# A transformer block on one core: layernorm tile 5 transposed by DMA, two tiles' statistics as sums, and a new order of the opening and the loop

## The chip, the cores and the metric

The kernel runs on one core of a Trainium2 chip. The time is the device time of one execution in microseconds; the median of three executions before the change is 274.92 us (274.09 to 275.06). The engines are called by their names or by the profile's short ones: TensorE (PE for matmuls, PEld for its weight loads), VectorE (DVE), ScalarE (ACT), GpSimd (POOL) and SyncE (SP), which here only issues DMAs.

## The reference

One block of a transformer over S = 2048 tokens of width D = 640, all in bf16: layernorm, a linear attention with 32 heads of width 20 and a softmax feature map, a residual, a second layernorm and a gated FFN of width 1536 with a second residual.

```python
def _A_ref(x, wqkv, w_phi, wo):
    qkv = ((x @ wqkv).reshape(B, S, 3, H, Dh)).transpose(2, 0, 3, 1, 4)
    q, k, v = qkv[0], qkv[1], qkv[2]
    pq = jnp.einsum("bhsd,hdf->bhsf", q, w_phi)
    pk = jnp.einsum("bhsd,hdf->bhsf", k, w_phi)
    phi_q = concat([softmax(pq), softmax(-pq)], axis=-1)
    phi_k = concat([softmax(pk), softmax(-pk)], axis=-1)
    kv = jnp.einsum("bhsf,bhsd->bhfd", phi_k, v)
    z  = jnp.einsum("bhsf->bhf", phi_k)
    num = jnp.einsum("bhqf,bhfd->bhqd", phi_q, kv)
    den = jnp.einsum("bhqf,bhf->bhq", phi_q, z)[..., None] + 1e-6
    return (num / den).transpose(0, 2, 1, 3).reshape(B, S, D) @ wo

h = x + _A_ref(layernorm(x), wqkv, w_phi, wo)
out = h + (gelu(layernorm(h) @ w_gate) * (layernorm(h) @ w_up)) @ w_down
```

## The kernel before

The tokens lie in 16 tiles of 128 (`t` = 0 to 15). Everything stays on the core; weights and x come in once, the result goes out once. The work of each engine, and of SyncE's DMA queue, stands in the order in which the kernel's calls are written: there is no planner. An engine does its own instructions strictly in that order and waits in front of each until its inputs are there; what is written earlier for another engine holds it only through data or through a buffer.

The stages, and the short names in which the calls are written:

- **Opening.** `load_x`, `load_v`, `load_phi`, `load_T` put x, the v weights, w_phi and the transposed q and k weights on SyncE's queue. `warm` and `warms` keep TensorE running on zeros. Tiles 0 to 2 are transposed with the mean taken off only (`c_sum`, `c_xc`, `c_sq`, `c_rstd`: the sum, the centred tile, the sum of squares, and rstd, which is put in later as a scale). Later tiles get `bn` (`bn_stats` of one half, with the aggregate after the second half), `rt` (rstd, on GpSimd with a power or on ScalarE with Ln and Exp), `mr` (minus mean times rstd), and `ap` (the normalized tile, on VectorE or ScalarE).
- **Transposes of the normalized tiles** into `LN1T`: `tr` makes five 128x128 transposes on TensorE into PSUM and `tc_` copies them out; `dt` instead puts one DMA transpose on SyncE's queue.
- **Folded weights.** `bd` makes the block diagonal of w_phi (`BD`); `fm(i, d)` multiplies chunk d of the q (i = 0) or k (i = 1) weights with it on TensorE, and `fc` casts the result into `Wq2` or `Wk2`.
- **Loop over the tiles.** `vm` makes v (ten matmuls of 128x320), `ve` evicts it; `km` makes pk, `ke(t, 0)` and `ke(t, 1)` its two exponentials on ScalarE; `ks` sums them per head on VectorE, `kr` takes the reciprocal, `kx(t, s, e)` scales v by it on VectorE ("v") or GpSimd ("g") into `vt`; `kv` adds 40 small matmuls per tile into the PSUM sum `kvp`. `kv_clear` builds a mask on GpSimd in pieces, `kv_mask` takes `kvp` out.
- **q side and attention.** `qm` and `qe` make the features of q; `ab`, `ae`, `a_den`, `a_rec`, `a_w`, `a_o` the attention of a tile; `o_tr`/`o_tc` or `o_dt` transpose it, `po_` projects it, `res` adds the residual.
- **FFN.** `gu`, `gl`, `gm` make gate and up, the GELU and their product, `dn` the down projection, `da` the last sum, `so` the store. `load_w` brings the weights for it.

Matmul results of all stages share four PSUM buffers. `gtile` hands them out in the order of the written calls, first freed first used, and `give` returns one after the call that reads it out. So which eviction a matmul group waits for follows from the written order of both. From the first `kv` to `kv_mask` one of the four holds `kvp`.

Lines 665 to 734 are the opening up to the second `bd`. VectorE's order there is: sums and centred tiles 0 to 2, the copies of tiles 0 and 1, `bn(3, 0)`, `bn(3, 1)`, the copy of tile 2 (`tc_(2, 0, 5)`), which `vm(2)` needs.

Of the kernel before, what the change touches and what calls it, by code (L numbers as in the profile page):

```python
# [8 lines left out]
BF16 = mybir.dt.bfloat16  # L9
# [8 lines left out]
def kernel(  # L18
# [76 lines left out]
    def eq_tiles(pool, j0, j1):  # L95
# [12 lines left out]
    tmean, trstd = (const.tile([P, 4], F32, name=n) for n in ("tmean", "trstd"))  # L108
# [16 lines left out]
    junk = fp.tile([P, D], BF16, name="junk")  # L125
# [6 lines left out]
    def col(x, t):  # L132
        return x[:, t:t + 1]
# [21 lines left out]
    def load_x(t0, t1):  # L155
        nc.sync.dma_start(x_sb[t0 // 4][:, t0 % 4:t0 % 4 + t1 - t0, :], x_v[:, t0:t1, :])  # L156
        have.update(("x", t) for t in range(t0, t1))
# [161 lines left out]
    def warmed():  # L319
        give(wu)  # L320
# [371 lines left out]
    load_x(10, 12)  # L692
    warm(0, 0)
# [40 lines left out]
    bd(3, 5, "g")  # L734
# [10 lines left out]
    vm(1, 4, 5)  # L745
    ve(1)
    vm(2)
    warmed()
    ap(3, "v")
    tr(3)  # L750
    bn(5, 0)
    bn(5, 1)
    rt(5, 1, "g")
    kv_clear(1)
    kv_clear(2)
    tc_(3, 0, 5, "v")
    bn(4, 0)
    bn(4, 1)
    ve(2)
    fm(1, 1)  # L760
    fc(1, 1, "a")
    fm(1, 0)
    fc(1, 0, "a")
    ap(5, "v")
    rt(4, 1, "a")
    ap(4, "v")
    vm(3)
    ve(3)
    tr(5)
    tc_(5, 0, 5, "v")  # L770
# [3 lines left out]
    fc(1, 3, "v")  # L774
    tr(4)
    fm(1, 4)
# [3 lines left out]
    tc_(4, 0, 5, "v")  # L780
    km(4)
    ke(4, 1)
    ke(4, 0)
    ke(0, 1)
    km(1)
    ke(0, 0)
    ke(1, 1)
    km(3)
    ke(3, 1)
    ke(1, 0)  # L790
    km(2)
# [36 lines left out]
    ke(7, 1)
    load_T(0, 4)
    dt(6)  # L830
    dt(9)
    load_T(0, 3)
    mr(8)
    ap(8, "a")
    km(5)
    ve(7)
    mr(10)
    ap(10, "a")
    dt(8)
    dt(10)  # L840
    vm(6, by_chunk=False)
    km(6)
    ke(7, 0)
    ke(5, 0)
    ve(6)
    ke(6, 0)
    vm(9, by_chunk=False)
    km(9)
    kr(0)
    kx(0, 1, "g")  # L850
    c_late(0, 3)
    ke(5, 1)
    mr(11)
    ks(2)
    kr(1)
    kx(1, 1, "g")
    kx(1, 0, "g")
    ve(9)
    ke(6, 1)
    kv(1)  # L860
    bn(12, 0, 2)
    bn(13, 0, 2)
    kr(2)
    bn(12, 1, 2)
    bn(14, 0, 2)
    bn(13, 1, 2)
    rt(12, 2, "g")
    kx(2, 0, "v")
    ap(0, "v")
    dt(0)  # L870
    load_T(0, 0)
    load_T(0, 2)
    load_T(0, 1)
    kx(0, 0, "g")
    kv(0)
    ke(9, 0)
    fm(0, 3)
    fc(0, 3, "a")
    ks(3)
    kr(3)  # L880
    kx(3, 0, "g")
    bn(15, 0, 2)
    ks(4)
    ks(5)
    kr(4)
    bn(15, 1, 2)
    mr(12)
    ap(12, "a")
    vm(8, by_chunk=False)
    ve(8)  # L890
    ke(9, 1)
    dt(12)
    kx(3, 1, "g")
    kx(2, 1, "g")
    kx(4, 1, "g")
    ap(13, "v")
    dt(13)
    km(8)
    ke(8, 1)
    ap(11, "a")  # L900
    dt(11)
    kr(5)
    bn(14, 1, 2)
    ks(6)
    kr(6)
    kx(6, 1, "v")
    kx(5, 0, "g")
    rt(14, 2, "g")
    mr(14)
    kx(5, 1, "g")  # L910
    kx(4, 0, "g")
    mr(15)
# [154 lines left out]
    load_w("o", 2, 5)  # L1067
# [507 lines left out]
```

## Time and profile before

| | |
|---|---|
| median of 3 runs | 274.92 us |
| the profiled execution's own time | 274.87 us |
| its span, first to last instruction | 273.2 us |
| granted TensorE clock | 1.000 |
| busy: VectorE, ScalarE, GpSimd | 178.1, 135.6, 89.3 us |
| DMA packets, bytes | 43392, 21.62 MB |

A page of the profile gives for each engine its busy time, then the span in 40 slices of 6.8 us with the busy share in tenths, then the chain of work that ended last, followed back from the last instruction. "A <- B" names what released an instruction. The time lines list instructions as start, length, engine, line, operation, output and inputs, shapes and count; what stands in brackets is the idle time in front and what ended it. Where "x2" stands, start and length are of both together.

### The profile page before, as it was taken

What the parts mean: (1) busy time and instruction counts of PE and PEld (TensorE: products, weight loads), DVE (VectorE), ACT (ScalarE), POOL (GpSimd) and SP (SyncE); (2) the same over time, 40 slices, a digit from 0 to 9 for tenths busy, and PEclk for the clock granted to TensorE, in tenths of its full rate; (3) what the DMA queues carried; (4) which work ended last, traced back from release to release, by engine and by line L of the source; (5) the groups of instructions that cost most, each with busy time, mean ns of one, the idle gap of its engine ahead of it and who ended that gap; (6) DMA issues with size and microseconds to landing.
All of it is one profiled execution on the core that took longest, in us unless ns stands there. A gap on an engine that the chain in (4) does not pass through costs nothing.

```text
span 273.2 us, 7140 instructions
## 1 busy us (share of the span) xinstructions
PE 268.7 (98%) x2981; PEld 171.0 (63%) x2981; DVE 178.1 (65%) x333; ACT 135.6 (50%) x236; POOL 89.3 (33%) x212
## 2 busy tenths in 40 slices
PE   8999999999999999999999999999999999999995
PEld 4777777766455887788755545675554576444574
DVE  6799999997586786676487855974457403233413
ACT  5968998859699665254704333422315340222200
POOL 4678999689003104342400320420201140000000
PEclk9999999999999999999999999999999999999999
DMA  6963878970780141321213021064001713000002
GB/s 199 198 236 75 118 101 90 230 282 2 234 303 3 26 28 26 73 52 24 52 26 96 2 48 27 0 124 50 0 0 48 122 48 97 2 0 1 24 2 96
DMA packets 43392, 21.62 MB, mean 79 GB/s; under 512 B 35936, under 2 KB 41312, under 8 KB 43360
## 3 DMA queue, kind: packets, MB, share of 16 engines
q1 hardware_dynamic: 43360, 21.17, 35.3%
q8 instruction: 23, 0.38, 0.6%
q14 instruction: 9, 0.07, 0.1%
HBM read 10.18 MB, written 2.62 MB: 47 GB/s over the span
## 4 chain that ended last, share of the span: by engine, by line
PE 95%; DMA 2%; SPq 1%; DVE 1%; issue 0%
PE gu L619 38%; PE pd L644 19%; PE pq L446 8%; PE po L546 8%; PE pk L377 8%; PE pv L330 7%; PE ab L491 2%; PE kvp L418 2%; DMA x_sb<-in_A_x_dram 2%; PE wa L356 1%; PE tp L150 1%; SPq L156 0%; DVE stats L260 0%; SPq L160 0%; DVE LN1T L130 0%
## 5 line engine op out<-in xcount | busy, mean ns | idle before, releaser
L625 ACT ACTIVATE g<-gu 128x512 bf16<-128x512 f32 (+1 forms) x60 | 29.7, 511 | 70.6 <-PE gu L619 70.1
L632 DVE TENSOR_TENSOR GT<-gu,g 128x512 bf16<-128x512 f32 (+1 forms) x60 | 33.9, 581 | 47.2 <-ACT g L625 47.2
L619 PE MATMUL gu<-LN2T,Wg 128*128 128x512 bf16 (+1 forms) x300 | 61.8, 337 | 0.0
L619 PE MATMUL gu<-LN2T,Wu 128*128 128x512 bf16 (+1 forms) x300 | 61.8, 337 | 0.0
L644 PE MATMUL pd<-Wd,GT 128*128 128x320 bf16 (+2 forms) x396 | 54.0, 296 | 0.0
L644 PEld LDWEIGHTS <-GT 128*128 128x128 bf16 x396 | 37.5, 98 | 14.3 <-DVE GT L632 0.3
L619 PEld LDWEIGHTS <-Wu 128*128 128x128 bf16 x300 | 29.3, 98 | 22.6
L619 PEld LDWEIGHTS <-Wg 128*128 128x128 bf16 x300 | 28.9, 98 | 22.0
L403 POOL TENSOR_TENSOR vt<-vS,rs 128x672 bf16<-128x672 bf16 x23 | 30.3, 1344 | 4.3 <-DVE rs L397 4.0
L654 DVE TENSOR_TENSOR y<-pd,x_sb 128x640 bf16<-128x640 f32 (+3 forms) x18 | 13.1, 744 | 23.5 <-PE pd L644 23.4
L524 DVE TENSOR_TENSOR tt<-AB,w 128x1280 bf16<-128x1280 f32 x16 | 23.8, 1490 | 1.2 <-POOL w L518 0.9
L546 PE MATMUL po<-Wo,oT 128*128 128x320 bf16 x160 | 24.2, 300 | 0.0
L330 PE MATMUL pv<-Wv,LN1T 128*128 128x320 bf16 x160 | 24.0, 300 | 0.1
L377 PE MATMUL pk<-Wk,LN1T 128*128 128x320 bf16 x160 | 23.4, 300 | 0.0
L446 PE MATMUL pq<-LN1T,Wq 128*128 128x512 bf16 x100 | 23.3, 380 | 0.0
L393 DVE TENSOR_REDUCE sk<-E 128x64 f32<-128x1280 bf16 x16 | 22.9, 1451 | 0.3 <-ACT E L384 0.3
L450 ACT ACTIVATE Eq<-pq 128x1024 bf16<-128x1024 f32 (+1 forms) x26 | 20.0, 851 | 4.9 <-PE pq L446 4.9
L580 POOL TENSOR_SCALAR v<-sm 128x1 f32<-128x1 f32 x14 | 4.9, 348 | 53.3 <-DVE x_sb L567 51.4
L546 PEld LDWEIGHTS <-oT 128*128 128x128 bf16 x160 | 15.5, 98 | 6.9 <-ACT oT L130 0.2
L130 ACT COPY AB<-ab 128x704 f32<-128x704 f32 x19 | 13.6, 743 | 12.4 <-DVE tt L524 9.8
L384 ACT ACTIVATE E<-pk 128x640 bf16<-128x640 f32 x26 | 17.4, 712 | 4.2 <-PE pk L377 3.2
L330 PEld LDWEIGHTS <-LN1T 128*128 128x128 bf16 x160 | 15.3, 98 | 6.6 <-DVE LN1T L130 0.7
(104 smaller groups left out, 286.9 us busy)
## 6 DMA issues: line engine op xcount, KB each, us to landing
out_dram<-y SPq DMA_DIRECT2D x15, 160.0 KB, 2.0
x_sb<-in_A_x_dram SPq DMA_DIRECT2D x6, 320.0 KB, 4.7
Wu<-in_B_w_up_dram SPq DMA_DIRECT2D x5, 384.0 KB, 8.2
Wg<-in_B_w_gate_dram SPq DMA_DIRECT2D x5, 384.0 KB, 4.6
Wd<-in_B_w_down_dram SPq DMA_DIRECT2D x4, 480.0 KB, 8.0
x_sb<-in_A_x_dram SPq DMA_DIRECT2D x4, 160.0 KB, 3.2
Wv<-in_A_wqkv_dram SPq DMA_DIRECT2D x2, 320.0 KB, 4.4
Wo<-in_A_wo_dram SPq DMA_DIRECT2D x1, 480.0 KB, 8.0
```

Source lines behind the costliest of these rows:

```text
L330: nc.tensor.matmul(pv[t][:, u, 0:HD], lhsT=lnT(t, c), rhs=Wv[:, c, u * HD:(u + 1) * HD], start=(c == 0), stop=(c == NC - 1))
L377: nc.tensor.matmul(pk[t][:, u, 0:HD], lhsT=lnT(t, c), rhs=Wk2[:, c, u * HD:(u + 1) * HD], start=(c == 0), stop=(c == NC - 1))
L393: nc.vector.reduce_sum(sk[t], Ek[t].rearrange("p s (h f) -> p (s h) f", f=Dh), axis=AX.X)
L403: E[e].tensor_tensor(Vt[t][:, s], vS[t % 8], rs[t][:, s * H:(s + 1) * H, None].to_broadcast([P, H, VC]), ALU.mult)
L446: nc.tensor.matmul(pqs[j][:, i, :], lhsT=Wq2[:, kc, c * P:(c + 1) * P], rhs=LN1T[b][:, kc, :], start=(kc == 0), stop=(kc == NC - 1))
L450: nc.scalar.activation(Eq[j][:, :, s, :], pqs[j][:, 0:len(QG[j])], ACTF.Exp, scale=(1.0, -1.0)[s])
L524: nc.vector.tensor_tensor(tt.rearrange("p s (h f) -> p s h f", f=Dh), num, w[t][:, :, :, None].to_broadcast([P, 2, H, Dh]), ALU.mult)
L546: nc.tensor.matmul(po[t][:, u, 0:HD], lhsT=oT[t][:, c, :], rhs=Wo[:, c, u * HD:(u + 1) * HD], start=(c == 0), stop=(c == NC - 1))
L619: nc.tensor.matmul(p[:, i, 0:a1 - a0], lhsT=W[:, c, f * P:(f + 1) * P], rhs=LN2T[b][:, c, a0:a1], start=(c == 0), stop=(c == NC - 1))
L625: nc.scalar.activation(x[:, 0:a1 - a0], p[:, 0, 0:a1 - a0], ACTF.Gelu_apprx_tanh)
L632: nc.vector.tensor_tensor(GT[b, f][:, a0:a1], p[:, 1, 0:a1 - a0], x[:, 0:a1 - a0], ALU.mult)
L644: nc.tensor.matmul(pd[k][:, u, n0:n1], lhsT=GT[b, f][:, tl * P:(tl + 1) * P], rhs=Wd[:, f, u * HD + n0:u * HD + n1], start=(f == 0), stop= ...
```

## The change

Four things change. Tile 5 is transposed by DMA (`dt(5)`) and no longer on TensorE. The statistics of tiles 12 and 13 come from a sum (ScalarE for 12, VectorE for 13) and a sum of squares on ScalarE, with a new function `sr` on GpSimd for their mean and rstd; the small buffers for it become 16 columns wide, and `junk`, which these passes write, moves to the pool `p1`. The second part of `bd` moves from GpSimd to VectorE. And the calls from there to the first `gu` stand in a new order for all engines, some on another engine. Nothing else of the computation changes.

The tiles and the new function:

```diff
-    tmean, trstd = (const.tile([P, 4], F32, name=n) for n in ("tmean", "trstd"))
+    tmean, trstd = (const.tile([P, NT], F32, name=n) for n in ("tmean", "trstd"))
...
+    junk = p1.tile([P, D], BF16, name="junk")
     tsum, tsq, tlog, nrstd, prstd = (
-        p1.tile([P, 4], F32, name=n) for n in ("tsum", "tsq", "tlog", "nrstd", "prstd"))
+        p1.tile([P, NT], F32, name=n) for n in ("tsum", "tsq", "tlog", "nrstd", "prstd"))
...
-    junk = fp.tile([P, D], BF16, name="junk")
...
+    def sr(t0, t1):
+
+        need(*(("sq", t) for t in range(t0, t1)))
+        n = t1 - t0
+        ve, rstd = small(p1, [P, n], "ve1"), small(p1, [P, n], "rstd1")
+        nc.gpsimd.tensor_scalar(ve, tsq[:, t0:t1], 1.0 / (D * D * D), EPS, op0=ALU.mult, op1=ALU.add)
+        nc.gpsimd.tensor_tensor(rstd, ve, nhalf[:, 0:n], op=ALU.pow)
+        nc.gpsimd.tensor_scalar(tmean[:, t0:t1], tsum[:, t0:t1], 1.0 / D, None, op0=ALU.mult)
+        for j in range(n):
+            lnp[t0 + j] = [col(tmean, t0 + j), rstd[:, j:j + 1], None]
```

The opening and the beginning of the loop, before and after, one call after the other (calls on one line stand in this order):

```diff
-    bd(3, 5, "g")
+    bd(3, 5, "v")
     c_sq(2); c_rstd(2, 3); bn(3, 0); bn(3, 1); rt(3, 1, "a"); tr(2); tc_(2, 0, 5, "v")
     vm(0, 2, 4); vm(0, 4, 5); ve(0); vm(1, 4, 5)
-    ve(1); vm(2); warmed(); ap(3, "v"); tr(3); bn(5, 0); bn(5, 1); rt(5, 1, "g")
-    kv_clear(1); kv_clear(2); tc_(3, 0, 5, "v"); bn(4, 0); bn(4, 1); ve(2)
-    fm(1, 1); fc(1, 1, "a"); fm(1, 0); fc(1, 0, "a"); ap(5, "v"); rt(4, 1, "a"); ap(4, "v")
-    vm(3); ve(3); tr(5); tc_(5, 0, 5, "v"); fm(1, 2); fc(1, 2, "a"); fm(1, 3); fc(1, 3, "v")
-    tr(4); fm(1, 4); fc(1, 4, "a"); km(0, True); loop_pools(); tc_(4, 0, 5, "v")
-    km(4); ke(4, 1); ke(4, 0); ke(0, 1); km(1); ke(0, 0); ke(1, 1); km(3); ke(3, 1)
-    ke(1, 0); km(2); ke(2, 1); vm(4); ve(4); ke(2, 0); bn(7, 0); bn(7, 1); bn(6, 0)
+    warmed(); bn(5, 0); ap(3, "v"); bn(5, 1); bn(4, 0); ve(1); vm(2); ve(2); bn(4, 1)
+    rt(4, 1, "a"); fm(1, 0); fc(1, 0, "v"); ap(4, "v"); tr(3); tc_(3, 0, 5, "v")
+    fm(1, 1); fc(1, 1, "a"); fm(1, 2); fc(1, 2, "a"); fm(1, 3); fc(1, 3, "a")
+    tr(4); tc_(4, 0, 5, "v"); kv_clear(1); kv_clear(2); bn(7, 0); bn(7, 1); bn(6, 0)
+    rt(5, 1, "g"); ap(5, "v"); rt(7, 1, "g"); dt(5); bn(6, 1); rt(6, 1, "g"); kv_clear(3)
+    ap(7, "v"); bn(8, 0, 2); bn(9, 0, 2); bn(8, 1, 2); dt(7); kv_clear(4); ap(6, "v")
+    bn(9, 1, 2); rt(8, 2, "g"); mr(8); mr(9); fm(1, 4); fc(1, 4, "a"); km(0, True)
+    loop_pools(); ke(0, 1); ke(0, 0); ks(0); km(2); ke(2, 1); ke(2, 0); km(1); ke(1, 1)
+    ke(1, 0); km(4); ke(4, 1); c_sum(12, "a"); vm(4); ve(4); ke(4, 0); ks(1); kr(1)
+    kx(1, 1, "g"); km(3); ke(3, 0); c_sq(12); ap(8, "a"); ke(3, 1); vm(3); ap(9, "a")
...
```

The rest of the loop after the change, engine by engine (the orders that the text refers to):

```
TensorE: km(5) vm(5) km(7) fm(0,3) vm(6) vm(7) km(6) fm(0,1) km(9) fm(0,4) kv(0) kv(1) kv(2) vm(9)
         km(8) km(10) vm(10) km(13) vm(13) kv(3) kv(4) kv(5) vm(12) vm(8) km(12) vm(11) km(11)
         kv(6) kv(7) vm(15) fm(0,2) km(15) vm(14) fm(0,0) km(14) qm(2) qm(0) kv(9) kv(8) kv(12)
         qm(3) qm(1) kv(15) kv(10) kv(13) kv(11) kv(14) qm(4) ab(0)
VectorE: ... bn(9,1) ks(0) ks(1) kr(1) bn(10,0) bn(11,0) bn(11,1) bn(10,1) ks(2) kr(0) kr(2) c_sum(13)
         fc(0,3) bn(14,0) ks(4) bn(15,0) ks(3) ap(13) kr(4) bn(15,1) ks(5) kr(3) bn(14,1) kr(5) ks(7)
         ap(0) ks(9) ks(8) kx(4,1) kx(5,1) kr(7) ks(6) kr(8) kr(9) kr(6) ap(1) ks(13) ks(10) ks(12) ...
GpSimd:  ... mr(8) mr(9) kx(1,1) kx(1,0) rt(10) mr(10) kx(0,0) kx(2,1) sr(12,14) kx(0,1) kx(2,0) mr(11)
         mr(12) kx(4,0) c_late kx(3,0) kx(5,0) rt(14) kx(3,1) mr(14) mr(15) kx(7,1) kx(7,0) kx(9,1)
         kx(6,1) kx(6,0) kx(9,0) ...
ScalarE: ... ve(5) ve(3) ke(5) c_sq(13) ap(10) ve(6) ve(7) ke(7) fc(0,1) ke(9) fc(0,4) ap(12) ke(6) ve(9) ...
SyncE:   x loads, dt(5) dt(7) load_T(0,3) dt(6) load_w(g,3,4) load_w(u,0,1) load_T(0,1) load_T(0,4)
         dt(8) dt(9) load_w(g,2,3) load_w(o,2,5) dt(10) dt(13) dt(12) load_w(u,2,3) dt(0) load_T(0,2)
         dt(11) load_w(u,1,2) load_T(0,0) dt(15) dt(14) dt(1) load_w(g,1,2) dt(2) load_w(u,4,5)
         load_w(u,3,4) load_w(o,0,2) load_w(g,4,5) load_w(d,3,6) load_w(g,0,1) o_dt(2) load_w(d,9,12)
         load_w(d,6,9) load_w(d,0,3)
```

The two x loads of tiles 12 to 15 are written before the loop now; on SyncE's queue they stood directly behind the other x loads already. In the attention stage `a_den(1)` goes from VectorE to GpSimd, the two evictions of `ab(0)` and of `ab(3)` change engines with one another, and `ab(3)` stands ahead of the first `gu`.

More of the change, by code (lines that the diff above doesn't have):

```diff
@@ L773 @@
     fm(1, 3)
-    fc(1, 3, "v")
+    fc(1, 3, "a")
     tr(4)
+    tc_(4, 0, 5, "v")
+    kv_clear(1)
+    kv_clear(2)
+    bn(7, 0)
+    bn(7, 1)
+    bn(6, 0)
+    rt(5, 1, "g")
+    ap(5, "v")
+    rt(7, 1, "g")
+    dt(5)
+    bn(6, 1)
+    rt(6, 1, "g")
+    kv_clear(3)
+    ap(7, "v")
+    bn(8, 0, 2)
+    bn(9, 0, 2)
+    bn(8, 1, 2)
+    dt(7)
+    kv_clear(4)
+    ap(6, "v")
+    bn(9, 1, 2)
+    rt(8, 2, "g")
+    mr(8)
+    mr(9)
     fm(1, 4)
@@ L846 @@
+    ap(13, "v")
+    dt(10)
+    kx(2, 0, "g")
+    mr(11)
+    mr(12)
+    ap(12, "a")
     ke(6, 0)
+    kv(1)
+    kv(2)
     vm(9, by_chunk=False)
[L848 to L870 removed]
@@ L885 @@
[L885 to L888, printed above, removed]
+    bn(14, 1, 2)
+    kr(5)
+    kx(5, 0, "g")
+    ks(7)
+    rt(14, 2, "g")
+    ap(0, "v")
+    dt(12)
+    load_w("u", 2, 3)
+    dt(0)
+    kx(3, 1, "g")
+    mr(14)
+    kv(3)
+    ks(9)
+    ks(8)
+    kx(4, 1, "v")
+    kv(4)
+    kx(5, 1, "v")
+    kv(5)
+    ke(13, 1)
+    ke(13, 0)
+    vm(12, by_chunk=False)
+    mr(15)
+    ap(15, "a")
+    ve(13)
+    ve(12)
+    ap(14, "a")
     vm(8, by_chunk=False)
     ve(8)
-    ke(9, 1)
```

449 lines of the change are left out of this document (209 added, 240 removed).

## The prediction

> **What bounds the kernel now.** I read the page first (busy times and the 40 slices), then the list of who waited for whom on TensorE, then the chain of waits in order of time, and last the time lines of VectorE, ScalarE, GpSimd and SyncE over the opening and the loop.
>
> ```profile
> PE 268.7 (98%) x2981; PEld 171.0 (63%) x2981; DVE 178.1 (65%) x333; ACT 135.6 (50%) x236; POOL 89.3 (33%) x212
> PE   8999999999999999999999999999999999999995
> PEclk9999999999999999999999999999999999999999
> ```
>
> The last wait of TensorE in the list of waits:
>
> ```profile
> PE ab L491 <- issue: 0.2, 1, 0.2
> ```
>
> TensorE is busy in every slice, at full granted clock, and after its start it waited once, 0.2 us in the attention stage. A busy TensorE need not be at its peak, so the chain of waits has to confirm it.
>
> ```profile
> 3.17 4.76 DMA x_sb<-in_A_x_dram
> ...
> 7.95 0.90 DVE stats L260 x2
> ...
> 9.08 0.36 DVE LN1T L130
> ...
> 9.49 1.53 PE pv L330 x10
> 11.03 0.28 PE tp L150 x5
> 11.30 0.65 PE wa L356 x12
> 11.95 1.47 PE pv L330 x10
> ...
> 14.65 0.32 PE wa L356 x6
> 14.97 6.79 PE pk L377 x50
> ...
> 33.99 0.79 PE kvp L418 x73
> 34.78 0.42 PE wa L356 x6
> 35.20 1.36 PE pv L330 x10
> ```
>
> Up to 9.49 us the start hangs on the load of x tile 3, its two `bn_stats` and the copy of tile 2. From there the chain stays on TensorE to the end: ten 128x320 matmuls take 1.36 us again and again, with no gap. So a microsecond that TensorE loses in the opening is lost for good, and another engine that gets faster gives nothing. What the edit can gain is TensorE work taken away, and that is five transposes (0.28 us).
>
> The other engines have little to spare in the loop:
>
> ```profile
> 20.00:30.00 10.00, 10.00 (x75) 7.21 (x74) 9.83 (x21) 9.30 (x14) 9.04 (x24) 1.00 0.52 71
> 30.00:40.00 10.00, 10.00 (x153) 7.31 (x151) 9.83 (x16) 9.77 (x18) 9.40 (x10) 1.00 0.75 113
> 40.00:50.00 10.00, 10.00 (x230) 7.49 (x229) 9.76 (x14) 8.52 (x17) 7.05 (x10) 1.00 0.88 164
> ```
>
> The columns are stretch, length, then busy time (count) of PE, PEld, DVE, ACT and POOL. VectorE is busy for 29.4 of these 30 us.
>
> **The change, part by part. The opening** is where I see the price. These are VectorE's rows of before, whose start-to-start distances I use, and GpSimd's row of `bd`:
>
> ```profile
> 8.19 1.67 POOL L210 TENSOR_TENSOR BD<-wphi,hmask 128x480 bf16<-128x480 bf16 x2 [0.17 <-DMA wphi<-in_A_w_phi_dram]
> ...
> 11.75 0.87 DVE L260 BATCH_NORM_STATS2 stats<-x_sb 128x6 f32<-128x320 bf16 x2
> 12.66 0.21 DVE L262 BATCH_NORM_AGGREGATE mv<-stats 128x2 f32<-128x12 f32 x1
> 12.79 0.40 DVE L289 TENSOR_SCALAR ln<-x_sb,mv,rstd 128x640 bf16<-128x640 bf16 x1
> 13.55 0.45 DVE L289 TENSOR_SCALAR ln<-x_sb,mv,rstd 128x640 bf16<-128x640 bf16 x1 [0.37 <-ACT rstd L271]
> 13.92 0.48 DVE L130 COPY LN1T<-tp 128x640 bf16<-128x640 bf16 x1
> 14.37 0.82 DVE L130 CAST Wk<-wa 128x640 bf16<-128x640 f32 x1
> 15.11 0.48 DVE L130 COPY LN1T<-tp 128x640 bf16<-128x640 bf16 x1
> ...
> 55.06 1.31 POOL L403 TENSOR_TENSOR vt<-vS,rs 128x672 bf16<-128x672 bf16 x1
> 55.11 1.98 DVE L403 TENSOR_TENSOR vt<-vS,rs 128x672 bf16<-128x672 bf16 x1
> ...
> 61.47 0.80 DVE L403 TENSOR_TENSOR vt<-vS,rs 128x672 bf16<-128x672 bf16 x1
> 61.51 1.94 POOL L403 TENSOR_TENSOR vt<-vS,rs 128x672 bf16<-128x672 bf16 x1
> ```
>
> `bd(3, 5)` moves to VectorE, in front of `bn(3)` and the copy of tile 2 that `vm(2)` waits for. No row shows it there. The nearest is the free `vt` of 672 elements, 0.80 us; 320 elements in proportion give 0.38, and I take 0.4. It cannot start before w_phi has landed, just ahead of 8.19, so `bn(3)` starts at about 8.55 in place of 7.95 and `vm(2)` at 10.1 in place of 9.49. The lower bound is 0.2 us (half, if two bf16 operands run faster): 9.9. The upper bound comes from the last four rows. A VectorE `vt` that starts 0.05 us after a GpSimd one ends 0.72 us after it, and in the second pair GpSimd waits instead: two such instructions do not overlap. Here GpSimd's `bd(0, 3)` waits for the same load; its two parts share the 1.67 us by elements as about 1.0 and 0.7. If GpSimd gets through first, VectorE begins at about 9.2 and `vm(2)` at 11.1. I take VectorE first: in the chain it follows the landing of x within 0.02 us.
>
> The Trainium skill says the same in "GPSIMD Engine Reference", § Key points: GpSimd shares its SBUF interfaces with VectorE, with contention for instructions that read two SBUF inputs. By that rule, which these four rows bear out, one of the two `bd` waits here; it does not say which.
>
> From the copy of tile 2 on, VectorE has `bn(5,0)`, `ap(3)`, `bn(5,1)`, `bn(4)`, `fc(1,0)`, `ap(4)`, `tc_(3)`. By the rows a `bn_stats` is 0.44, one with its aggregate 0.60, `ap` 0.37, the cast of Wk 0.74, a copy 0.45. So `fc(1,0)` ends 3.2 us and `tc_(3)` 4.0 us after `vm(2)` starts (call that s). TensorE has in that time `vm(2)` 1.53, `fm(1,0)`, `tr(3)`, `fm(1,1)`, `fm(1,2)`: some 2.8 us. Handing out the four PSUM buffers in program order, `fm(1,3)` gets the one that `fc(1,0)` frees and `tr(4)` the one that `tc_(3)` frees. TensorE therefore waits about 0.4 us for the first and 0.5 for the second, and with `tr(4)` 0.28 and `fm(1,4)` 0.32 it reaches `km(0)` at s + 4.6 = 14.7. Before, it got there at 14.97 with `vm(3)` already done, which now stands in the loop for 1.36. The price is 14.7 + 1.36 - 14.97 = **1.1 us** (0.9 with the lower bound, 2.1 with the upper). `tr(5)`, which is gone, is inside this sum. Nothing hides it: every TensorE piece from here on is work.
>
> **Tile 5 by DMA.** Its copy on VectorE and five transposes go; one transpose joins SyncE's queue ahead of the one of tile 7.
>
> ```profile
> 11.85 2.48 SPq L156 DMA_DIRECT2D x_sb<-in_A_x_dram  x5
> ...
> DMA to landing us min/median/max: 2.6/2.6/5.1
> ```
>
> The second row is that of the 13 transposes of tiles. All the x loads leave in one row at 11.85 already, so that two are written earlier changes nothing on the queue. `bn(7)` started at 15.5 before without a wait, so its data is there then; `ap(5)` ends near 17.4, and the transpose, 5.1 us at most, lands by 22.6. `km(5)`, its first reader, comes at 14.7 + 7 x 1.36 = 24.2. Cost 0; were the cover gone it would be up to 5 us.
>
> The Trainium skill ("VectorE: DVE Perf Modes", § The three transpose paths) speaks against this edit: 1309 ns for a 128x128 block by DMA against 390 ns on TensorE. An estimate from that page, five blocks in a row, is 6.5 us and would still land just before `km(5)`; the trace's 2.6 us for the whole tile disagrees with a row of five and decides.
>
> **Loop, VectorE.** Four `bn_stats` and two aggregates go (2.1), the sum of tile 13 comes, as do two more `vt` on VectorE (1.6; 9 become 11, GpSimd's go from 23 to 21), and `fc(0,3)`.
>
> ```profile
> 3.11 0.82 DVE L223 TENSOR_REDUCE tsum<-x_sb 128x1 f32<-128x640 bf16 x1 [0.79 <-DMA x_sb<-in_A_x_dram]
> ...
> 22.22 2.83 DVE L393 TENSOR_REDUCE sk<-E 128x64 f32<-128x1280 bf16 x2
> 24.96 0.54 DVE L397 RECIPROCAL rs<-sk 128x64 f32<-128x64 f32 x1
> ...
> 30.04 1.29 ACT L384 ACTIVATE E<-pk 128x640 bf16<-128x640 f32 x2
> ```
>
> Net it gains about 1.2 us of work (0.8 + 1.6 + 0.9 for `fc(0,3)` as two half casts + 0.4 for `bd`, less 2.1 and the 0.45 of `tc_(5)`), as `fc(1,0)` only takes the place of `fc(1,3)`. The point where this can reach TensorE is `kv(5)`, which reads `kx(5,1)`. From `bn(7)` at 15.5 VectorE has to do 16 `bn_stats` and their aggregates 8.3, five `ap` 2.1, nine `ks` at 1.37 12.3, six `kr` at 0.46 2.8, the sum 0.8, `fc` 0.9, two `vt` 1.6: 28.8, so 44.3. TensorE reaches `kv(5)` at 14.7 + 30.3 = 45.0 (20 blocks of 1.36, three `fm`, five `kv` at half of 0.79, and switches). The slack is 0.7 us. GpSimd then makes five `vt` of 1.31 and ends `kx(6,0)` near 51.4; `kv(6)` comes at 52.3. ScalarE, which gains the squares of 12 and 13 and the sum of 12, is nearest at `vm(9)`: it waits for both exponentials of tile 9, 1.29 us, and TensorE has `fm(0,4)` and three `kv`, some 1.5, in between. So by these sums the loop costs 0, with slacks of 0.2 to 0.8 us; one missed by a port wait or a late semaphore costs some tenths. I add **0.1**.
>
> **Blocks of `kv`.** The `fm` right after a block of `kv` takes 0.42 where others take 0.32. The new order has five such blocks for six: **-0.1**.
>
> **Weights and attention.**
>
> ```profile
> 68.74 0.38 SPq L173 DMA_DIRECT2D Wd<-in_B_w_down_dram  x1
> ...
> 88.44 1.09 PE gu L619 x10
> ...
> Wd<-in_B_w_down_dram SPq DMA_DIRECT2D x4, 480.0 KB, 8.0
> ```
>
> The last part of the gate weights now stands behind the first of Wd, which can leave only when the loop's tiles are free, at about 70. With 8 us each to land it is there by 80, ahead of the first `gu` at 88 to 90. Three Wd parts now wait behind the transpose of `o(2)`; their first reader is the down projection far behind. In the attention one denominator moves to GpSimd. I cost these at 0.
>
> The sum: +1.1 + 0.1 - 0.1 = +1.1 on the profiled execution's 274.87 us (span 273.2 and 1.67 around it), which is 0.05 under the median of 274.92. That gives **276.0**.
>
> **The rivals.** *The port is lost*: GpSimd's `bd` gets through first. For it: both wait for one load, and 55.06 shows GpSimd winning by 0.05 us. Against: VectorE has been quicker to follow a landing. It adds 1.0: 277.0. *The loop starves at the `kv`*: VectorE's `kx(4,1)` meets GpSimd's `kx(3,1)`, as at 55.11, and loses up to 1.2 us. It decides from 0.7 us of lateness on at `kv(5)`; what is over is lost, and `kx(6,0)`, which follows on GpSimd, carries it to `kv(6)`, together 0.5 to 1.5: 276.5 to 277.5. For it speaks a VectorE at 98% in these stretches; against, GpSimd is done with `kx(3,1)` by the same rows at 37.1 (`kr(3)`) + 3 x 1.31 + about 1 for the rstd of 14 = 42.0, and VectorE gets to `kx(4,1)` at 42.7. *Not slower*: VectorE's chain of the opening does not hold TensorE. `bd` takes 0.2, and VectorE frees the two PSUM buffers before TensorE asks for them, that is, it needs 2.8 us from the copy of tile 2 to `tc_(3)` in place of 4.0. Then `km(0)` comes after TensorE's own work alone, 9.9 + 1.53 + five `fm` of 0.32 and two `tr` of 0.28 = 13.6, with `vm(3)` at 15.0 as before, and the sum is -0.1: 274.8. Against it: those are seven instructions of kinds that all have rows here, and only the one of `bd` has none. *The edit doesn't do what it says* is excluded for the order, which is written by hand.
>
> **How the numbers follow.** The forecast (opening alone, 275.6 to 276.4) has 0.48, the starved loop 0.25, the lost port 0.12, not slower 0.15. A difference of 0.5%, 1.37 us, is about what a measurement here can tell from no change; that bound lies at 276.3. Slower by more: all of the lost port, four fifths of the starved loop and a fifth of the forecast's own spread, 0.12 + 0.20 + 0.10 = 0.42. Faster by more would need 273.5, which even the third rival misses: 0.03. The rest, 0.55, is within. The range goes from 274.7 to 277.5: it holds the third rival's upper half and all but the tail of the starved loop.
>
> **What would show it.** `vm(2)` at about 10.1 with VectorE's `bd` at 8.15 to 8.6 ahead of `bn(3)`; TensorE idle for 0.4 us ahead of `fm(1,3)` (waiting for the cast of Wk on VectorE) and 0.5 ahead of `tr(4)` (for the copy of LN1T); `km(0)` at 14.7; no wait of TensorE between there and the last `kv`; no wait for the DMA of tile 5. A `km(0)` by 13.9 would prove the opening wrong; a wait at `kv` the loop; a wait of the first `gu` for a DMA the weights.

## The result, and the profile after

| | before | after |
|---|---|---|
| median of 5 runs on one chip (lowest to highest) | 274.92 (274.09 to 276.54) | 276.69 (276.31 to 277.45) |
| ratio after / before, 95% interval | | 1.0070 (1.0047 to 1.0094) |
| the profiled execution's own time, its span | 274.87, 273.2 | 276.53, 274.8 |

The changed kernel is slower by 1.8 us in the medians and by 1.66 us in the two profiled executions. The granted clock is 1.000 in both. (Of all runs below only two of e2's, at 278.6 us, had one under 0.998, namely 0.994; without them e2's median would be 276.1.) The ratio comes from all runs and isn't the quotient of the medians. The page's busy times of the kernel after:

```profile
PE 269.0 (98%) x2976; PEld 171.6 (62%) x2976; DVE 179.8 (65%) x330; ACT 137.4 (50%) x240; POOL 87.3 (32%) x212
```

Five transposes are gone from TensorE (2976 matmuls for 2981), yet its busy time is 269.0 us for 268.7: one row of several matmuls can hold a wait, as will be seen. The 1.6 us that the span gained are waits. The list of who waited for whom on TensorE, kernel after (total, times, longest):

```profile
PE wu L324 <- DVE zero L679: 1.2, 1, 1.2
PE pv L341 <- DVE LN1T L130: 0.9, 1, 0.9
PE ab L502 <- issue: 0.3, 1, 0.3
PE tp L150 <- DVE LN1T L130: 0.3, 1, 0.3
```

The wait of 1.2 us is that for the zeros at the start, which every kernel here has. The two for `LN1T` are in the opening: `vm(2)` waits for VectorE's copy of tile 2, and `tr(4)` for its copy of tile 3. The chain of waits of the kernel after (start, length, what):

```profile
3.68 3.91 DMA wphi<-in_A_w_phi_dram
...
7.68 1.33 DVE BD L210
9.01 0.81 DVE stats L271 x2
...
10.05 0.37 DVE LN1T L130
...
10.46 1.54 PE pv L341 x10
...
12.09 0.80 ACT vS L348
...
13.39 0.44 DVE ln L300
13.83 0.41 DVE LN1T L130
...
14.29 0.44 PE tp L150 x5
14.72 0.32 PE wa L367 x6
15.04 5.43 PE pk L388 x40
...
35.00 1.42 PE kvp L429 x110
...
68.36 1.74 PE kvp L429 x184
```

The start no longer hangs on x tile 3 but on the load of w_phi and on VectorE's `bd(3, 5)`. `vm(2)` starts at 10.46 (9.49 before), `km(0)` at 15.04 (14.97 before). In the chain a piece starts where the one in front ends; the time lines below give `km(0)`'s first matmul, 14.88 here and 14.81 before. The last block of `kv` starts at 68.36. In the chain of the kernel before that is

```profile
66.81 1.74 PE kvp L418 x183
```

so 1.55 of the span's 1.6 us are lost by then, and behind it these two executions differ by next to nothing. Of the 1.55, the opening is 15.04 + 1.36 (`vm(3)`, still to do) - 14.97 = 1.43.

The time line of the kernel after, at `bd`, at `fm(1,1)` to `fm(1,3)` and at the first `kv` (start, length, engine, line, operation, shapes, count, idle time in front):

```profile
7.67 0.99 POOL L210 TENSOR_TENSOR BD<-wphi,hmask 128x480 bf16<-128x480 bf16 x1
7.68 1.33 DVE L210 TENSOR_TENSOR BD<-wphi,hmask 128x320 bf16<-128x320 bf16 x1 [0.31 <-DMA wphi<-in_A_w_phi_dram]
...
12.42 1.58 PE L367 MATMUL wa<-BD,WkT 128*128 128x140 bf16 x18
...
33.10 2.67 POOL L414 TENSOR_TENSOR vt<-vS,rs 128x672 bf16<-128x672 bf16 x2
...
34.93 1.49 PE L429 MATMUL kvp<-vt,E 128*32 128x42 bf16 x120
...
44.61 1.19 PE L429 MATMUL kvp<-vt,E 128*32 128x42 bf16 x120
```

The two halves of `bd` start 0.01 us apart, and VectorE's, the smaller one, ends last, 0.35 us after GpSimd's (9.01 and 8.66). That is the rival "the port is lost". The 18 matmuls of the three `fm` take 1.58 us, where three of 0.32 are 0.96: the other 0.6 us are nearly all waits inside the row. The last two rows are blocks of three `kv` each, and the first is 0.30 us longer. GpSimd ends the pair `kx(0,1)`, `kx(2,0)` at 35.77, and `kv(2)`, the third of the first block, needs the second of them; its turn would be at 34.93 + 2 x 0.40 = 35.73. So GpSimd is done just when TensorE asks, at the latest possible moment. The block's matmuls come more slowly from 35.3 on, so not all of the 0.30 us is a wait for `kx(2,0)`; what the rest is stays open.

### The profile page after: what moved, and what is told of

The parts are those of the page before. It is cut to its first block, busy times and chain, and to the rows that moved or that the text cites. A ratio compares the mean times of both kernels' runs of the same rounds, so it can differ in the third digit from the quotient of the medians.

```text
span 274.8 us, 7134 instructions
## 1 busy us (share of the span) xinstructions
PE 269.0 (98%) x2976; PEld 171.6 (62%) x2976; DVE 179.8 (65%) x330; ACT 137.4 (50%) x240; POOL 87.3 (32%) x212
## 4 chain that ended last, share of the span: by engine, by line
PE 94%; DMA 1%; DVE 1%; SPq 1%; ACT 0%; issue 0%; DVEq 0%; ACTq 0%
PE gu L630 38%; PE pd L655 19%; PE pq L457 8%; PE po L557 8%; PE pk L388 8%; PE pv L341 7%; PE ab L502 2%; PE kvp L429 2%; DMA wphi<-in_A_w_phi_dram 1%; PE wa L367 1%; SPq L156 1%; PE tp L150 1%; DVE BD L210 0%; SPq L160 0%; DVE stats L271 0%
## 5 line engine op out<-in xcount | busy, mean ns | idle before, releaser
L414 POOL TENSOR_TENSOR vt<-vS,rs 128x672 bf16<-128x672 bf16 x21 | 27.9, 1354 | 4.2 <-DVE rs L408 4.2
L557 PEld LDWEIGHTS <-oT 128*128 128x128 bf16 x160 | 15.5, 98 | 6.9 <-ACT oT L130 0.3
```

The source lines that it names most:

```text
L414: E[e].tensor_tensor(Vt[t][:, s], vS[t % 8], rs[t][:, s * H:(s + 1) * H, None].to_broadcast([P, H, VC]), ALU.mult)
L557: nc.tensor.matmul(po[t][:, u, 0:HD], lhsT=oT[t][:, c, :], rhs=Wo[:, c, u * HD:(u + 1) * HD], start=(c == 0), stop=(c == NC - 1))
```

## The experiments

All times are medians in us; the last column is one execution's: how much later than in the kernel before (66.74 in its time line) the last block of `kv` starts. "Over before" is against the kernel before in the same series on the same chip (274.92 for the first row, 274.72 for e1 to e4, 274.62 for e5 to e8, 274.66 for e9 to e12).

| run | edit | median | over before | ratio (95%) | last `kv` |
|---|---|---|---|---|---|
| after | the whole change | 276.69 | +1.8 | 1.0070 (1.0047 to 1.0094) | +1.55 |
| e2 | before, `bd(3, 5)` on VectorE | 276.32 | +1.6 | 1.0071 (1.0042 to 1.0099) | +1.79 |
| e1 | after, `bd(3, 5)` on GpSimd | 276.13 | +1.4 | 1.0054 (1.0035 to 1.0074) | +2.92 |
| e3 | after, GpSimd's `bd(0, 3)` later | 276.10 | +1.4 | 1.0048 (1.0035 to 1.0061) | +1.11 |
| e4 | e1, `bn(5)` later | 275.98 | +1.3 | 1.0047 (1.0035 to 1.0059) | +1.05 |
| e5 | e4, `sr` and `ap(13)` later | 275.95 | +1.3 | 1.0041 (1.0028 to 1.0053) | +1.48 |
| e6 | the opening of before, the loop of after | 275.51 | +0.9 | 1.0025 (1.0015 to 1.0035) | +0.96 |
| e8 | e6, `sr` and `ap(13)` later | 275.13 | +0.5 | 1.0023 (1.0014 to 1.0033) | +0.68 |
| e9 | e8, x tiles 6 and 7 one place earlier | 275.05 | +0.4 | 1.0014 (1.0001 to 1.0027) | +0.56 |
| e7 | before, tile 5 by DMA | 274.83 | +0.2 | 1.0008 (0.9997 to 1.0020) | -0.12 |
| e10 | e8, `kx(5, 1)` on GpSimd | 275.98 | +1.3 | 1.0048 (1.0030 to 1.0066) | +1.26 |
| e11 | e5, `kx(5, 1)` on GpSimd | 276.67 | +2.0 | 1.0066 (1.0048 to 1.0084) | +1.41 |
| e12 | e10, tile 5 by DMA | 276.63 | +2.0 | 1.0069 (1.0053 to 1.0086) | +2.10 |

Behind that block single executions still differ: from its start to the q matmuls behind `ab(0)` it is 4.81 us in the kernel before and 4.40 in e7, which has the same code there; the 0.4 us are a stall at the first `ab`, whose cause is open.

### e2: the step of `bd` alone

The kernel before with

```diff
-    bd(3, 5, "g")
+    bd(3, 5, "v")
```

> The kernel before with only the second part of bd moved to VectorE. Port theory: 0.9 to 1.1 us slower than before, 275.8 to 276.0, with vm(2) at about 10.4 and VectorE's bd at 1.3 us. Rival (the rest of the new order is what costs): within 0.3 us of before.

This one word costs 1.6 us, nearly as much as the whole change, and more than the 1.1 us that I had expected at most. The time line of e2 and, below it, its chain of waits:

```profile
8.30 0.99 POOL L210 TENSOR_TENSOR BD<-wphi,hmask 128x480 bf16<-128x480 bf16 x1 [0.17 <-DMA wphi<-in_A_w_phi_dram]
...
8.32 1.32 DVE L210 TENSOR_TENSOR BD<-wphi,hmask 128x320 bf16<-128x320 bf16 x1 [0.52 <-DMA wphi<-in_A_w_phi_dram]
```

```profile
3.68 4.54 DMA wphi<-in_A_w_phi_dram
...
8.32 1.32 DVE BD L210
...
11.08 1.53 PE pv L330 x10
```

Here too GpSimd gets through first. `vm(2)` starts at 11.08, which is the prediction's upper bound of 11.1 and 1.59 us later than before. In the kernel after it was 10.46 only because w_phi had landed 0.6 us earlier in that execution (`bd` starts at 7.68 and at 8.32).

### e1, e3, e4: the same step taken out of the change

e1 is the kernel after with

```diff
-    bd(3, 5, "v")
+    bd(3, 5, "g")
```

> The changed kernel with the second part of bd back on GpSimd, all else as changed. Port theory (VectorE's bd of 1.33 us is mostly a wait for GpSimd's bd, and all of it is lost): VectorE starts bn(3) when x tile 3 lands, vm(2) comes 0.9 to 1.0 us earlier than in the changed kernel (about 9.5 in place of 10.46), and the time falls by as much, to 275.6 to 275.9. Rival (bd is hidden behind the rest of VectorE's and ScalarE's opening, which the new order made long): under 0.3 us of gain, 276.4 or more.

e3 is the kernel after with GpSimd's half out of VectorE's way:

```diff
-    bd(0, 3, "g")
     bd(3, 5, "v")
     c_sq(2)
     c_rstd(2, 3)
+    bd(0, 3, "g")
```

> The changed kernel with GpSimd's part of bd one step later, behind the small prstd of tile 2, so that VectorE's part meets a free port. Port theory: VectorE's bd takes 0.35 to 0.4 us in place of 1.33, and the time falls by 0.5 to 0.9 us to 275.8 to 276.2. Rival (a product of two broadcast operands is that slow on VectorE by itself): bd stays at 1.2 us or more and the time at 276.7.

e4 is e1 with tile 5's statistics out of the opening's chain:

```diff
-    bn(5, 0)
     ap(3, "v")
-    bn(5, 1)
...
     tc_(4, 0, 5, "v")
+    bn(5, 0)
+    bn(5, 1)
```

> As the first run (bd on GpSimd), and the two bn of tile 5 behind the copy of tile 4, where VectorE stood idle for 0.7 us waiting for x. If VectorE's chain from the copy of tile 2 to that of tile 3 holds TensorE, TensorE's waits ahead of fm(1,3) and tr(4) shrink from some 0.8 us to 0.4 or less, and the time is 0.3 to 0.6 us under the first run's, about level with or 0.4 us under before (274.5 to 275.2). If TensorE is held by ScalarE's evictions there, no gain over the first run.

e3 shows what the instruction costs with a free port. Its time line:

```profile
8.22 0.49 DVE L210 TENSOR_TENSOR BD<-wphi,hmask 128x320 bf16<-128x320 bf16 x1 [0.61 <-DMA wphi<-in_A_w_phi_dram]
...
9.25 0.99 POOL L210 TENSOR_TENSOR BD<-wphi,hmask 128x480 bf16<-128x480 bf16 x1
```

0.49 us, start to next start 0.41, where it was 1.33 beside GpSimd. So the wait for the port is 1.33 - 0.49 = 0.8 us. But the three kernels come down by only 0.4 to 0.5 us (over before, +1.8 to +1.4 and +1.3): the 1.6 us that `bd` costs alone can't be had back here. For e1 that is less than its theory's 0.8 us or more, and e4, for which I expected 0.3 to 0.6 us under e1, came 0.15 under it. Something else holds the time up as soon as the opening is quicker.

The traces show two things. The first is a load again. With `bd(3, 5)` back on GpSimd, TensorE waits for the k weights of `fm(1,3)`; e1's list of waits has

```profile
PE wa L367 <- DMA WkT<-in_A_wqkv_dram: 0.8, 1, 0.8
```

and e4, e5 and e11 have 0.2, 1.1 and 0.4 us there. In e1, where the weights for v and x tile 3 came late too, this leaves `km(0)` at 14.96, no earlier than in the kernel after.

The second is in the loop. In these kernels VectorE works without a gap from `bn(7)`, the first work on x tiles 6 and 7, into the loop, and GpSimd without a gap from `rt(6)`, which waits for VectorE's statistics of tile 6. ScalarE's `ap(8)` needs GpSimd's `mr(8)`. ScalarE's and TensorE's rows of e1, the execution in which these tiles came latest, with VectorE's `bn(7)` first:

```profile
17.42 0.89 DVE L271 BATCH_NORM_STATS2 stats<-x_sb 128x6 f32<-128x320 bf16 x2 [2.22 <-DMA x_sb<-in_A_x_dram]
...
26.44 0.92 ACT L298 ACTIVATE ln<-x_sb,mr,rstd 128x640 bf16<-128x640 bf16 x1 [1.62 <-POOL mr L292]
...
28.00 1.52 PE L388 MATMUL pk<-Wk,LN1T 128*128 128x320 bf16 x10 [0.65 <-ACT E L395]
...
37.30 0.47 PE L429 MATMUL kvp<-vt,E 128*32 128x42 bf16 x40 [0.32 <-POOL vt L414]
```

`ap(8)` waits 1.62 us for `mr(8)`, the exponentials behind it on ScalarE are late, `km(7)` waits for them, and `kv(2)` waits for GpSimd's `kx(2,0)`. The same starts in the kernel after and in these three, from their time lines; `vm(9)` is the first work behind `kv(0)` to `kv(2)`:

| | `km(0)` | `bn(7)` | `ap(8)` | `vm(9)` | `ap(8)` - `bn(7)` | `vm(9)` - `bn(7)` | `vm(9)` - `km(0)` |
|---|---|---|---|---|---|---|---|
| after | 14.88 | 15.97 | 24.98 | 36.35 | 9.01 | 20.38 | 21.47 |
| e1 | 14.96 | 17.42 | 26.44 | 37.70 | 9.02 | 20.28 | 22.74 |
| e3 | 14.57 | 15.45 | 24.47 | 35.92 | 9.02 | 20.47 | 21.35 |
| e4 | 14.23 | 15.58 | 24.58 | 35.83 | 9.00 | 20.25 | 21.60 |

`ap(8)` keeps its distance from `bn(7)` to 0.02 us (it is 9.00 in e5 and e11 as well) and `vm(9)` to 0.2 us, while the distance from `km(0)` differs by 1.4 us. GpSimd's pair `kx(0,1)`, `kx(2,0)` ends 19.80, 19.83, 19.83 and 19.79 us after `bn(7)`. So where TensorE stands at the end of the third `kv` is set, in these four executions, by the landing of x tiles 6 and 7 and by the work of VectorE and GpSimd behind it, not by TensorE's opening. (In e6 below, whose opening has done tile 5's statistics earlier, that pair ends 19.22 us after `bn(7)`.)

Most of this distance is GpSimd's own queue. The kernel after, GpSimd's `rt(6)` and `rt(8)` and, between them, the end of VectorE's statistics of tiles 8 and 9:

```profile
18.54 0.30 POOL L284 TENSOR_SCALAR ve<-mv 128x1 f32<-128x1 f32 x1 [0.32 <-DVE mv L273]
...
20.94 0.21 DVE L273 BATCH_NORM_AGGREGATE mv<-stats 128x2 f32<-128x12 f32 x1
...
23.55 0.23 POOL L284 TENSOR_SCALAR ve<-mv 128x2 f32<-128x2 f32 x1
```

By these statistics `rt(8)` could have begun at 21.15. It starts 2.4 us later, as the 16 small mask instructions of `kv_clear(3)` and `kv_clear(4)`, 19.45 to 23.46, stand ahead of it. Not all of that could be had: `kx(1,1)`, behind it on GpSimd, needs VectorE's `kr(1)`, which ends at 24.48, and starts at 25.14. No run moved the masks, so what it would give isn't shown.

In the kernel after, the limit is 15.97 + 20.27 = 36.24 (20.27 from e1 and e4, where `kv(2)` waits), and TensorE came to 36.35: an opening quicker by any amount could have given 0.1 us with that landing. The delay in the opening and the limit of the loop are two causes of about the same size, one beside the other, and the later of the two counts. The sizes fit: `bd` alone costs 1.6 us (e2) and the loop alone 0.9 (e6, below), but both together 1.8, not 2.5. e4's chain of waits now runs over these engines:

```profile
12.05 3.51 DMA x_sb<-in_A_x_dram
...
15.58 0.90 DVE stats L271 x2
...
28.80 2.55 POOL vt L414 x2
...
32.74 2.65 POOL vt L414 x2
...
35.43 0.47 PE kvp L429 x36
```

Between the second and the third row shown the chain goes over VectorE up to 27.42, where GpSimd's `rt(10)` follows the sum `ks(2)`. But `rt(10)` doesn't read that sum, and in e8 it starts at 27.11, ahead of that sum's end at 27.57. In both it starts 0.09 us behind GpSimd's own pair in front, so this step, too, is GpSimd's queue.

e1 is no clean measure of the undoing: its profiled execution was the slowest of its six (277.69 against a median of 276.13), with `bn(7)` 1.45 us later than in the kernel after.

### e6, e8, e9, e5: the loop

e6 is the kernel after with the calls of the kernel before from `bd(3, 5)` to `km(0)`, of which the core is

```diff
-    bd(3, 5, "v")
+    bd(3, 5, "g")
...
+    vm(3)
+    ve(3)
+    tr(5)
+    tc_(5, 0, 5, "v")
...
-    rt(5, 1, "g")
-    ap(5, "v")
...
-    dt(5)
...
-    vm(3)
...
-    ve(3)
```

> The opening of the kernel before up to km(0) (bd on GpSimd, tile 5 on TensorE, vm(3) ahead of the loop), then the changed order of the loop and everything behind it, with the statistics of tiles 6 to 9 directly behind the opening. Theory of two bounds in parallel: GpSimd's chain does not care for TensorE's opening and kx(2,0) ends at 35.4 to 35.8 as in the changed kernel, TensorE gets to kv(2) at about 34.6 and waits 0.7 to 1.0 us, so the kernel stays 0.6 to 1.0 us slower than before (275.3 to 275.7). Rival (the whole price lies in the opening, as the prediction had it, the loop costs 0): 274.5 to 274.8.

e8 changes this in e6, and e5 changes it in e4:

```diff
-    sr(12, 14)
...
-    ap(13, "v")
+    kr(4)
+    bn(15, 1, 2)
+    ks(5)
     dt(10)
     kx(2, 0, "g")
+    sr(12, 14)
+    ap(13, "v")
...
-    kr(4)
...
-    bn(15, 1, 2)
-    ks(5)
```

> The run e4 (bd on GpSimd, bn of tile 5 later), and in the loop sr of tiles 12 and 13 (1.26 us of GpSimd) behind kx(2,0) in place of ahead of kx(0,1), with VectorE's ap(13) behind ks(5). Theory: with the opening cured the next bound is GpSimd's queue from the landing of x tiles 6 and 7 to kx(2,0), which kv(2) waits for. Then kx(2,0) ends 1.3 us earlier, TensorE's wait of 0.3 us there goes, and the time falls 0.3 to 0.5 us under e4, to 275.5 to 275.7. Rival (the rest of e4's excess over before lies elsewhere, in ScalarE or the attention): no change from e4, 276.0.

> The run e6 with sr behind kx(2,0) and ap(13) behind ks(5), as in e5. Theory of two bounds: both are gone, kx(2,0) ends near 34.3, ahead of TensorE, and the time is level with before (274.5 to 274.9). Rival (something else of the new loop costs): it stays at that of e6.

e9 is e8 with

```diff
-    load_T(1, 4)
     load_x(6, 8)
+    load_T(1, 4)
```

> The run e8 (opening of before, new loop, sr later) with the load of x tiles 6 and 7 one place earlier on SyncE's queue, ahead of the last transposed chunk of the k weights. Theory (VectorE's queue runs without a gap from the landing of x tile 6, near 15.8 in e8, to kx(5,1), which kv(5) waits for): the landing and everything behind it on VectorE come 0.5 to 1.0 us earlier, the wait of 0.2 us at kv(5) goes, and the time falls 0.1 to 0.3 us unless fm(1,4) now waits for its weights. Rival (VectorE is bound by ScalarE's exponentials, not by x): kx(5,1) ends where it did in e8, 44.5, and the time stays at 275.1.

With the opening of before the change costs 0.9 us (e6): that is the price of the loop by itself, where I had put 0. e6's list of waits, but for the zeros:

```profile
PE pv L341 <- DMA Wv<-in_A_wqkv_dram: 0.4, 1, 0.4
PE kvp L429 <- POOL vt L414: 0.3, 1, 0.3
```

The first is a load of the opening (`km(0)` starts 0.14 us later than before), the second is `kv(2)`. `sr(12, 14)`, three small instructions for tiles 12 and 13, stands on GpSimd ahead of `kx(0,1)` and `kx(2,0)` and delays them by 1.4 us (e4's two pairs of `vt` start 3.94 us apart, and the first takes 2.55). In e8, behind them, the wait at `kv(2)` is gone, though the time, 275.13, stays over the 274.5 to 274.9 that I expected. The next wait is `kv(5)`, for VectorE's `kx(5,1)`, and the loop's statistics still show on ScalarE. From e8's time line:

```profile
15.87 0.89 DVE L271 BATCH_NORM_STATS2 stats<-x_sb 128x6 f32<-128x320 bf16 x2 [0.32 <-DMA x_sb<-in_A_x_dram]
...
29.22 0.83 ACT L234 ACTIVATE junk<-x_sb,tsum 128x640 bf16<-128x640 bf16 x1 [0.61 <-DVE tsum L223]
...
44.61 0.31 PE L429 MATMUL kvp<-vt,E 128*32 128x42 bf16 x20 [0.17 <-DVE vt L414]
```

ScalarE's square for tile 13 waits 0.61 us for VectorE's sum of tile 13, and the evictions of v behind it come later. It starts 13.35 us after `bn(7)` here, and just so in e6 (15.98, 29.33), e10 (15.89, 29.24) and e12 (16.74, 30.09): again the landing of x plus VectorE's work. e9 has x tiles 6 and 7 land earlier (`bn(7)` at 15.50, without a wait), and all three waits are gone from its lists; the block of `kv(3)` to `kv(5)` is still 0.14 us longer than its usual 1.19. From `km(0)` to the last `kv` e9 takes 52.07 us, where the kernel before takes 51.93 and e8 52.66: with x tiles 6 and 7 there 0.8 us earlier as seen from `km(0)`, this loop costs 0.1 us. In their place stands the load that it was put ahead of:

```profile
PE wa L367 <- DMA WkT<-in_A_wqkv_dram: 0.3, 1, 0.3
```

So `km(0)` starts at 15.23 for e8's 14.76, and the median is only 0.1 us under e8's, which the intervals don't tell apart. The loads leave SyncE's queue one after the other, and both are wanted as early as they come.

e5, the same delay of `sr` with the new opening, did not come under e4 (275.95 and 275.98). Its `vm(9)` came 19.86 after `bn(7)`, 0.4 nearer than in e4, but `bn(7)` came 0.50 later (16.08), and `fm(1,3)` waited 1.1 us for its weights.

### e7: tile 5 by DMA alone

The kernel before with

```diff
-    tr(5)
-    tc_(5, 0, 5, "v")
+    dt(5)
```

> The kernel before with tile 5 alone transposed by DMA: five transposes and one copy out of PSUM go, one DMA transpose joins SyncE's queue behind the x loads. Theory (TensorE's work sets the end, the DMA lands well ahead of vm(5)): 0.2 to 0.3 us faster than before, at 274.4 to 274.5. Rival (the transpose lands late because x loads are in front of it): a wait of TensorE for LN1T at vm(5) and 275 or more.

No wait of TensorE names this transpose. `km(0)` starts 0.09 us earlier; the time lines of before and, below it, of e7:

```profile
14.81 6.96 PE L377 MATMUL pk<-Wk,LN1T 128*128 128x320 bf16 x50
...
14.72 6.95 PE L377 MATMUL pk<-Wk,LN1T 128*128 128x320 bf16 x50
```

Of this, 0.08 us were there already at `vm(3)`, in front of the edit (11.81 for 11.89). `fm(1,2)` then starts 0.36 us earlier (13.18 for 13.54), but `tr(4)` waits 0.19 us for VectorE's `ap(4)`, and `km(0)` starts 0.45 us behind `fm(1,4)` for 0.32: what the transposes left free is filled by waits.

The ratio of 1.0008 (0.9997 to 1.0020) doesn't show the 0.28 us: they are 0.1%, inside the interval's half width. Here `dt(5)` leaves ahead of the x loads of tiles 12 to 15, in the kernel after behind them. The DMA costs nothing that can be measured, and gains nothing that can be.

### e10, e11, e12: the wait at kv(5), and a miss

e10 is e8, and e11 is e5, with

```diff
-    kx(5, 1, "v")
+    kx(5, 1, "g")
```

> The run e8 with kx(5,1) on GpSimd, which stood idle for 2.1 us at that point, in place of VectorE. Theory (VectorE's queue is what kv(5) waits for): kv(5) doesn't wait, kr(7) comes 0.8 us earlier, and the time falls 0.2 to 0.4 us to 274.7 to 274.9, level with before. Rival (the 0.2 us wait is all, or the new order's excess lies behind the loop): 275.1.

> The run e5 (the changed kernel with bd on GpSimd, bn of tile 5 later, sr later) with kx(5,1) on GpSimd. If three bounds lie one behind the other (the port, GpSimd's queue, VectorE's queue), this run is the first with the new opening in which all are gone: 0.2 to 0.5 us under e5, 275.4 to 275.7, what is left being the new opening's wait for tile 3's copy. Rival: still 275.9, held by late landings of the opening's loads.

e12 is e10 with

```diff
-    tr(5)
-    tc_(5, 0, 5, "v")
+    dt(5)
```

> The run e10 with tile 5 transposed by DMA: the opening of before without its five transposes, the new loop with its two waits cured. TensorE has 0.3 us less to do than before and no wait is known: 274.3 to 274.6, level with before or 0.1% under it. Rival (the new loop has a further wait): 274.9 or more.

In e8 GpSimd has 2.1 us without work where VectorE does `kx(4,1)` and `kx(5,1)`, so I moved the second there. It was meant to gain 0.2 to 0.4 us; the kernel got slower by 0.8 us (e10 against e8). e10's time line:

```profile
42.77 1.31 POOL L414 TENSOR_TENSOR vt<-vS,rs 128x672 bf16<-128x672 bf16 x1
...
42.97 1.82 DVE L414 TENSOR_TENSOR vt<-vS,rs 128x672 bf16<-128x672 bf16 x1
...
44.06 0.86 POOL L292 TENSOR_SCALAR mr<-mv,rstd 128x1 f32<-128x1 f32 x1
...
44.85 0.66 PE L429 MATMUL kvp<-vt,E 128*32 128x42 bf16 x60 [0.74 <-DVE vt L414]
```

GpSimd's `vt` starts 0.20 us before VectorE's and VectorE's ends 0.71 us after it, as in the two rows at 55.06 and 55.11 that the prediction shows. `kv` waits 0.74 us where it waited 0.17. This is the prediction's second rival, with `kx(5,1)` in place of `kx(3,1)`, made by my own edit. It explains 0.58 us, by which the last `kv` comes later than in e8; the rest of e10's span lies behind it, where e10's list has the stall at `ab` (0.2) and e8's has not. e11 has the same wait (0.67 us) and e12 has it too, so neither tests its theory, which had this wait cured. In e12 x tiles 6 and 7 also landed 0.85 us later than in e10; `vm(9)` came 0.86 us later (36.08 and 35.22). Why all six runs of e12 lie above 276.0 with an edit that cost nothing in e7, and why e11's runs fall into two near 276.0 and four at 276.6 to 277.0, is open.

No kernel of these is faster than the one before.

## Why the prediction was right, and where it was not

The time of 276.69 lies in the range, 0.7 us over the forecast of 276.0. That is in part luck: w_phi landed early in the profiled execution, and the price of the opening covers one of the loop that I had at nothing. Point by point:

1. **What bounds the kernel: right.** Nearly all that was lost was lost by TensorE ahead of the last `kv`.
2. **`bd` on VectorE: the step that failed.** "I take VectorE first" was wrong. In both executions in which the halves met, GpSimd got through first, and in e2 `vm(2)` came at the upper bound (11.08). The guess rested on how soon VectorE follows a landing of x. I had seen the row that spoke for GpSimd (55.06) and gave that rival 0.12. The instruction's own price, 0.4 us, was right (0.41 in e3). The landing of w_phi differed by 0.6 us between executions, and it hid two thirds of the mistake in the kernel after: 10.46 for 10.1.
3. **The waits behind it: right in kind, 1.43 us for 1.1.** The forecast had TensorE idle 0.4 us ahead of `fm(1,3)` and 0.5 ahead of `tr(4)`. From `fm(1,1)` at 12.42 to `tr(4)` at 14.29 it is 1.87 us with 0.96 us of work, so 0.9 idle as forecast. The weight loads of `fm(1,2)` and `fm(1,3)` start at 12.94 and 13.53, just behind ScalarE's `ve(2)` (to 12.88) and VectorE's `fc(1,0)` (to 13.47): a wait for ScalarE that I hadn't seen seems to be among them. From `vm(2)` to `km(0)` it was 4.58 us, where I had 4.6. So the size was missed in the start of `vm(2)` alone. The chain of waits goes over ScalarE too (`ve(2)`, `rt(4)`, then `ap(4)`), but VectorE has no gap ahead of `ap(4)`: its own queue, as I had it, got there at the same time.
4. **Tile 5 by DMA at 0: right** (e7). But the 0.28 us that five transposes less should gain by point 1 didn't show either.
5. **The loop at 0: wrong, and hidden by point 2.** By itself it costs 0.9 us (e6), with 0.14 of it in the opening of that execution. My sum for VectorE was good: 28.8 us from `bn(7)` to the end of `kx(5,1)`; in the kernel after it is 29.0 (44.98 - 15.97). Two things failed. I took `bn(7)` to start at 15.5, as before, since "its data is there then"; it waited 0.71 us for the load and started at 15.97, and in other executions between 15.45 and 17.42. And I costed `kv(5)` and `kv(6)`, not `kv(2)`, for which GpSimd's queue with the masks and `sr` in it is the last to be ready, nor ScalarE's `ap(8)`, which hangs on that queue, and its square of tile 13, which hangs on VectorE's sum.
6. **The switch of `kv` blocks: not isolated.** From `km(0)` to the last `kv`, less `vm(3)`, it is 51.96 us after and 51.84 before; the 0.30 us of the longer first block are in that.
7. **Weights and attention at 0: right.** The first `gu` waits for no DMA, and the stall ahead of `ab` is 0.3 us for 0.2.

The Trainium skill's rule ("GPSIMD Engine Reference", § Key points) that GpSimd and VectorE contend for the shared interfaces bears on the largest single cost here. The traces agree, and they add that the loser all but waits out the other's instruction: in e2 and in the kernel after VectorE's `bd` ends 0.35 us behind GpSimd's, 0.8 us later than it would by itself.

## What to carry to other kernels

When two engines share a port and wait for the same load, price the one on the critical path as the loser (e2); an idle GpSimd is no free place for work beside VectorE's two-input instructions (e10). Before a delay is costed, compute when each other engine would have stopped TensorE anyway: two causes that run side by side don't add up, and undoing either shows little (e1, e3, e4). Measure such distances from the landing of the load that feeds the chain, not from the span's start; a distance that stays the same to some hundredths of a microsecond over several executions points to what a place hangs on, and the queue in between tells what could be moved out of it (here `sr` and the masks).

## What the runs showed of the hardware

**Single-input work of VectorE is held up too.** `ap` reads one tile. VectorE's time line of the kernel after, `ap(4)` while GpSimd has only small work, and `ap(13)` beside GpSimd's `vt` of 33.10:

```profile
13.39 0.44 DVE L300 TENSOR_SCALAR ln<-x_sb,mv,rstd 128x640 bf16<-128x640 bf16 x1
...
33.63 0.97 DVE L300 TENSOR_SCALAR ln<-x_sb,tmean,rstd 128x640 bf16<-128x640 bf16 x1
```

It took 0.97 us for 0.44. The other way round, GpSimd's 128x1 `mr` took 0.86 us beside VectorE's `vt` in e10, and 0.26 at 42.54, just ahead of the two `vt`.

**Loads land at very different times.** The same load of w_phi took 3.91 us from its issue in the kernel after and 4.44 in e3 (4.54 in e2). VectorE got x tiles 6 and 7 at 15.45 to 17.42. That is as large as the effects studied here.
